# Sixteen seven-product blocks instead of thirteen, eight-wide channel runs, and engine orders written as lists, in a convolution and GELU kernel

## The chip, the cores and the metric

One core of a Trainium2 chip runs the kernel. The core has a matrix engine (TensorE, "PE" in the profile, with weight loads as "PEld"), VectorE (DVE), ScalarE (ACT), GpSimd (POOL), and a sync engine (SP) that issues transfers. Each engine works through its own queue in order and waits on semaphores for the others. The metric is the device time of one execution in microseconds (us).

## The reference, cut to what matters

x has 8 sequences of 4096 rows with 192 channels. Eight heads of 24 channels have seven taps each, which are normalised by a softmax. A causal convolution along the rows is followed by a two-layer product with an exact GELU between the layers:

```python
w = exp(weight - max); w = w / (sum(w) + 1e-9)        # [8 heads, 7 taps]
conv[b, s, c] = sum_k w[head(c), k] * x_pad[b, s + k, c]   # 6 zero rows ahead
h = conv.reshape(32768, 192) @ w_in                   # 192 x 2048
out = gelu_exact(h) @ w_out                           # 2048 x 192
```

## The kernel before, in words

The 32768 rows are two halves of 16384, which are worked on side by side: partitions 0 to 63 hold channels of the first half, 64 to 127 those of the second. A partition holds three of the 192 channels (NP = 3). A half is cut into 35 blocks: six of 256 rows (0 to 5), then 29 of 512 rows (6 to 34). So `win` holds W_in with three rows per partition, and each product with it takes three matmuls.

For one block n the stages are these:

- SP loads x rows into `xin` (`load`), one of three buffers, and stores results (`store`). Its queue alternates: load of block n+4, store of block n-1.
- DVE turns `xin` into `xT`, channels on partitions, by 32x32 transposes (`trans`, L800). Partition j holds the channels 3j, 3j+1, 3j+2, so the transpose reads every third element of a row of `xin`. POOL copies the last six rows of the block before it into the head of `xT` (`halo`, L723).
- The convolution is seven taps over 128 x 1536 elements. Tap 0 is a plain scaling, in three pieces on ACT (`first_tap`, L938; blocks 7 and 8 have it on DVE). Taps 1 to 6 are DVE multiply-adds into `acc` (`conv`, L827). The last one writes `xc` in bf16.
- TensorE forms the first product, 16 slices of 128 hidden channels for both halves, into two PSUM buffers `hp` (`mm1`, L1066). Four quadrants of 64x64 run side by side.
- ACT applies GELU to each slice and writes `gT` (L974).
- TensorE forms the second product for block n-1, between the slices of the first product of block n. DVE transposes the result back into `osb`.

The second product has two forms for blocks 6 to 33. A plain block (`mm2_t`, L1150) multiplies two row halves and two chunk parities of `gT` with three groups of 64 output channels: 12 products of 16 matmuls of 512 columns, 192 in all. A seven-product block (the list ST, `mm2_s`, L1202) replaces the eight products of two of the output groups by seven (P1 to P7), of sums of `gT` and of weights; the third group has D1, D2, E1, E2 (with pieces e1, e2). Together that is 11 products. The sums S1, Dn and S4 are made by DVE in `st_add`, S3 partly by DVE and partly by accumulating DMA transfers (`st_dma`, L545), which POOL issues. S3 overwrites a quarter of `gT`. After the product, ACT copies pieces of the PSUM banks X, D, Y and V to SBUF (`st_copy`: p5, p1, e, u, p3, -u, -g), DVE combines them (`st_post`: k0, k3, k4) and transposes the result (`st_evac`: ev). The tiles for this are `p5s`, `gsm`, `uu` and `tq`. The four banks of `ob` are handed from block to block (`BK`, `release`).

In the kernel before, ST holds every other block from 9 to 33: 13 blocks, each between two plain ones. The order on TensorE inside a seven-product block comes from TILES, which gives each quadrant its products. EVENTS merges the four orders by the time that each takes, counted in products: 5.5 in all. Some matmuls are marked to raise a semaphore (DONE): the last one of a product, and those after which the other row half takes over the same bank (SWITCH).

The order on DVE is a plan of transposes and taps by block, with side work put between them at fixed places (`AT_ST`, `at_ev`). ACT's copies stand at fixed slices (`AT_COPY`), its first taps too (`TAPS`). DVE's plan for block n runs about while TensorE works on block n-1.

Of the kernel before, what the change touches and what calls it, by code (L numbers as in the profile page):

```python
# [5 lines left out]
ALU = mybir.AluOpType  # L6
# [5 lines left out]
def bass_lightweight_conv__then__act_gelu_exact_kernel(  # L12
# [42 lines left out]
    DQ = D // 2  # L55

# [15 lines left out]
    ST = [m for m in range(M0 + 3, M1) if m % 2 == 1]  # L72
    K0 = {n: i for i, n in enumerate([4, 5, 6, *range(9, NB)])}
# [48 lines left out]
    with es:  # L122
# [61 lines left out]
        S_K0 = sem("S_K0")  # L184
        S_WT = sem("S_WT")
        S_ST = sem("S_ST")
# [3 lines left out]
        S_AD = [sem("S_AD%d" % q) for q in range(2)]  # L190
# [50 lines left out]
        def wait_pc(e, n, p):  # L241
# [11 lines left out]
            n: [(0, 0, 2), (0, 2, 1)] * (n not in K0) + [(k, 0, NP) for k in range(1, KS)]  # L253
            for n in range(NB)
            if n not in PC
        }
        FQ = F // 8
# [55 lines left out]
        def wait_banks(t, m, g):  # L313

            k = G0[m] + g
            if m < M0:
                if k >= 2:
                    t.wait_ge(S_EVA, k - 1)
            elif g % 2:
                t.wait_ge(S_GELU, SL0[NB] - 1 + g // 2)  # L320
            else:
                for b in LAST[g : g + 2]:
                    t.wait_ge(*release(OWNER[b], b))
# [42 lines left out]
        def evac_t(v, m, j):  # L366
# [22 lines left out]
            (0, 0): "P1 D1 e2 e1 D2 P6 P2", (1, 0): "D1 P1 P2 e2 e1 D2 P6",  # L389
            (0, 1): "P5 P7 E2 E1 P4 P3", (1, 1): "E2 P7:2 P5 P7:6 P3 E1 P4",  # L390
# [3 lines left out]
        EVENTS = []  # L394
        for (hf, cg), names in TILES.items():
            at, done = 0.0, {}
            for u in names.split():
                u, k1 = (u.split(":") + ["8"])[:2]
                k0 = done.get(u, 0)
                d = SPAN.get(u, (0, TB))[1] / TB  # L400
                for k in range(k0, min(8, k0 + int(k1))):
                    EVENTS.append((at, hf, cg, u, k))
                    at += d / 8
                    done[u] = k + 1
            assert abs(at - 5.5) < 1e-6 and all(k == 8 for k in done.values())
        EVENTS.sort(key=lambda q: (round(q[0], 4), q[1], q[2]))
        GROUP = {}
        for e, (at, hf, cg, u, k) in enumerate(EVENTS):
            name = {"D": "DE", "E": "DE", "e": "Ea"}.get(u[0], u)
            GROUP[name] = e  # L410
        DONE = {GROUP[name] for name in NE}
        SWITCH, last = {}, {}
        for e, (at, hf, cg, u, k) in enumerate(EVENTS):
            p = last.get((UNIT[u][0], cg))
            if p is not None and EVENTS[p][1] != hf:
                SWITCH[e] = p
                DONE.add(p)
            last[UNIT[u][0], cg] = e
        FIRST = {}
        for e, (at, hf, cg, u, k) in enumerate(EVENTS):  # L420
            FIRST.setdefault((UNIT[u][0], cg), e)
        DONE.discard(len(EVENTS) - 1)
        DONE = sorted(DONE)
# [3 lines left out]
        def st_done(e, m, name):  # L427
            if GROUP[name] == len(EVENTS) - 1:
                e.wait_ge(S_MM2, MMC[m + 1])
            else:  # L430
                e.wait_ge(S_ST, len(DONE) * ST.index(m) + DONE.index(GROUP[name]) + 1)

        COPIES = ("p5", "p1", "e", "u", "p3", "-u", "-g")
        AT_COPY = {
            "p5": (1, 6), "p1": (1, 8), "e": (1, 14), "u": (2, 0), "p3": (2, 2), "-u": (2, 6), "-g": (2, 10),
        }

        def ac(m, name):

            return len(COPIES) * ST.index(m) + COPIES.index(name) + 1  # L440

        POSTS = ("k0", "k3", "k4")

        def dp(m, name):

            return len(POSTS) * ST.index(m) + POSTS.index(name) + 1

        SUMS = {"S1": (0, 4, 6, 8), "S3": (6, 8), "Dn": (0, 4, 8), "S4": (0, 4, 8)}

        def sa(m, name, k):  # L450

            return (len(SUMS[name]) - 1) * ST.index(m) + [k < q for q in SUMS[name][1:]].index(True) + 1

        AT_ST = [
            (2, 1, 0, "S1", 0), (2, 1, 2, "Dn", 0), (2, 1, 4, "S4", 0), (2, 1, 6, "S1", 1),
            (2, 2, 2, "S1", 2), (2, 2, 4, "S3", 0), (2, 3, 0, "Dn", 1), (2, 4, 0, "S4", 1),
            (2, 5, 0, "k0", 0), (3, 1, 0, "ev", 2),
            (3, 6, 0, "k3", 0), (4, 1, 1, "ev", 1), (4, 1, 5, "k4", 0), (4, 2, 0, "ev", 0),
        ]

        def at_ev(n):

            if n == M0:
                return [(3, 1, 3), (3, 2, 1), (3, 2, 3)]
            return [(3, 1, 3), (3, 2, 1), (3, 2, 3)]
# [3 lines left out]
        for n in range(M0, M1):  # L469
            if n not in ST:  # L470
                SIDE += [((n + at[0], *at[1:]), "ev", n, j) for j, at in enumerate(at_ev(n))]
            else:
                SIDE += [((n + d, o, r), name, n, q) for d, o, r, name, q in AT_ST]
        SIDE.sort(key=lambda q: q[0])
        EV = {}
        for _, name, n, j in SIDE:
            if name in ("ev", "evac"):
                EV[n, j] = EVC[M0 - 1] + len(EV) + 1

        def release(m, b):  # L480
# [4 lines left out]
            if k == "X":  # L485
                return S_AC, ac(m, "p3")
# [5 lines left out]
        for m in range(M0, M1):  # L492
            for b in BK[m].values() if m in ST else BK[m]:
# [819 lines left out]
```

## Time and profile before

| what | value |
| --- | --- |
| median of 3 runs | 669.04 us (668.91 to 669.47) |
| profiled execution | 667.87 us, its span 666.1 us |
| PE busy | 661.4 us, 99% of the span |
| DVE busy | 600.7 us, 90% |
| ACT busy | 610.8 us, 92% |
| POOL busy | 47.6 us, 7% |
| GELU on ACT (L974) | 510 of 1.022 us |
| DVE taps (L827, 128 x 1536, into acc) | 145 of 1.811 us |
| input transposes (L800, 128 x 1536) | 29 of 2.369 us |
| DMA engines, mean | 96 GB/s |

The span reaches from the first to the last instruction of the profiled execution. Busy time is the time in which an engine has at least one instruction under way, and an instruction's row gives its count and mean duration. Instructions of DVE and ACT overlap a little, so the start-to-start time can be less than the duration. "Idle before" names what ended the wait of an engine. In a row of TensorE by order of time, a group of 12 matmuls is one slice of the first product.

### The profile page before, as it was taken

Reading aid. Unit: us, or ns where it says so; the run is one execution under the profiler, and the core shown is the slowest. Engines: PE = TensorE matmul, PEld = TensorE weight load, DVE = VectorE, ACT = ScalarE, POOL = GpSimd, SP = SyncE. Lnnn points to the kernel's source line nnn. Section 1 sums busy time; section 2 is a strip of 40 time slices with the busy share of each in tenths; the row PEclk is TensorE's granted clock in tenths of the full one; section 3 lists DMA queues with packets and bytes.
Section 4 is the critical chain, followed back from the end, with each engine's and each line's share of the span. In section 5 each row is a group of like instructions: output and inputs, shape, how many; then the busy total and the mean of one; then the engine's idle time right before and its main releaser. Section 6 shows DMA issues by size and latency. Waiting matters only on the chain.

```text
span 666.1 us, 27567 instructions
## 1 busy us (share of the span) xinstructions
PE 661.4 (99%) x12712; PEld 516.4 (78%) x12712; DVE 600.7 (90%) x510; ACT 610.8 (92%) x720; POOL 47.6 (7%) x87
## 2 busy tenths in 40 slices
PE   8999999999999999999999999999999999999998
PEld 8999655557667787877878778787787878878787
DVE  6979999799999999999999999999999999999632
ACT  8999988889999999999999999999999999999884
POOL 7000000010000100001010010100001000010100
PEclk9999999999999999999999999999999999999999
DMA  9735334243081461905529073370824719151233
GB/s 159 165 89 130 65 69 97 72 93 79 18 197 29 107 135 34 203 7 127 114 41 201 3 163 78 62 179 2 191 50 91 151 29 192 22 118 29 56 90 97
DMA packets 137028, 63.92 MB, mean 96 GB/s; under 512 B 126800, under 2 KB 133520, under 8 KB 136912
## 3 DMA queue, kind: packets, MB, share of 16 engines
q1 hardware_dynamic: 129136, 49.37, 33.2%
q0 software_dynamic: 6656, 12.19, 10.1%
q8 instruction: 100, 1.64, 1.1%
q10 hardware_dynamic: 1120, 0.59, 0.3%
q14 instruction: 16, 0.13, 0.1%
HBM read 28.31 MB, written 25.17 MB: 80 GB/s over the span
## 4 chain that ended last, share of the span: by engine, by line
PE 99%; ACT 0%; DVE 0%; DMA 0%; issue 0%; ACTq 0%
PE hp L1066 50%; PE ob L1150 23%; PE ob L1202 18%; PE ob L1106 5%; PE ob L1258 1%; PE hp L1258 1%; PE ob L1011 0%; DMA wsb<-in_weight_dram 0%; PE ob L1066 0%; ACT dg L912 0%; DVE wcol L772 0%; ACT xc L237 0%; ACT osb L347 0%; ACT wex L899 0%; ACT xTb L269 0%
## 5 line engine op out<-in xcount | busy, mean ns | idle before, releaser
L974 ACT ACTIVATE gT<-hp 128x1024 bf16<-128x1024 f32 x510 | 513.0, 1022 | 43.0 <-PE hp L1066 35.7
L1066 PE MATMUL hp<-xc,win 64*64 64x512 bf16 (+2 forms) x6036 | 438.4, 366 | 0.2
L1066 PEld LDWEIGHTS hp<-xc,win 64*64 64x64 bf16 (+1 forms) x6036 | 247.2, 106 | 73.0 <-ACT gT L974 4.6
L827 DVE SCALAR_TENSOR_TENSOR acc<-xT,wcol,acc 128x1536 f32<-128x1536 f32 (+1 forms) x165 | 282.9, 1714 | 10.6 <-ACT acc L938 7.3
L1150 PE MATMUL ob<-gT,wot 64*64 64x512 bf16 x2880 | 205.6, 376 | 0.0
L1202 PE MATMUL ob<-gT,wot 64*64 64x512 bf16 x832 | 158.0, 376 | 0.0
L1150 PEld LDWEIGHTS ob<-gT,wot 64*64 64x64 bf16 x2880 | 112.1, 107 | 43.3
L1202 PE MATMUL ob<-gT,wst 64*64 64x512 bf16 (+2 forms) x832 | 144.0, 323 | 0.0
L1202 PE MATMUL ob<-s_S,wot 64*64 64x128 bf16 (+2 forms) x624 | 89.9, 305 | 0.0
L800 DVE STREAM_TRANSPOSE xT<-xin 128x1536 f32<-128x1536 f32 (+2 forms) x39 | 76.2, 1963 | 3.8 <-DMA xin<-in_x_dram 1.4
L1202 PEld LDWEIGHTS ob<-gT,wst 64*64 64x64 bf16 x832 | 68.5, 107 | 10.7
L1202 PEld LDWEIGHTS ob<-gT,wot 64*64 64x64 bf16 x832 | 63.9, 107 | 1.5
L938 ACT ACTIVATE acc<-xT,wcol 128x512 f32<-128x512 f32 (+1 forms) x87 | 61.2, 703 | 0.0
L827 DVE SCALAR_TENSOR_TENSOR xc<-xT,wcol,acc 128x1536 bf16<-128x1536 f32 (+1 forms) x33 | 56.7, 1720 | 0.8
L1202 PE MATMUL ob<-s_S,wst 64*64 64x512 bf16 x208 | 57.4, 376 | 0.0
L1202 PE MATMUL ob<-s_Dn,wst 64*64 64x512 bf16 x208 | 57.4, 376 | 0.0
L1202 PEld LDWEIGHTS ob<-s_S,wot 64*64 64x64 bf16 x624 | 50.2, 107 | 8.6
L545 POOL DMA_DIRECT2D gT<-gT x26 | 22.4, 861 | 318.1 <-DVE s_S L559 318.1
L1106 PE MATMUL ob<-wout,gT 64*128 64x192 bf16 x768 | 41.9, 243 | 0.0
L1106 PEld LDWEIGHTS ob<-wout,gT 64*128 64x128 bf16 x768 | 35.1, 94 | 3.3
L373 DVE STREAM_TRANSPOSE osb<-ob 128x512 f32<-128x512 f32 x45 | 31.1, 694 | 6.2 <-PE ob L1150 6.2
L559 DVE TENSOR_TENSOR s_S<-gT 128x1024 bf16<-128x1024 bf16 (+1 forms) x39 | 32.6, 837 | 1.4 <-ACT gT L974 1.3
(78 smaller groups left out, 322.6 us busy)
## 6 DMA issues: line engine op xcount, KB each, us to landing
out_dram<-osb SPq DMA_DIRECT2D x124, 192.0 KB, 3.6
xin<-in_x_dram SPq DMA_DIRECT2D x116, 192.0 KB, 4.2
gT<-gT POOLq DMA_DIRECT2D x13, 512.0 KB, 4.6
gT<-gT POOLq DMA_DIRECT2D x13, 256.0 KB, 3.3
xin<-in_x_dram SPq DMA_DIRECT2D x18, 96.0 KB, 2.5
wout<-in_moe_w_out_dram POOLq DMA_DIRECT2D x4, 192.0 KB, 4.7
win<-in_moe_w_in_dram POOLq DMA_DIRECT2D x4, 96.0 KB, 4.3
win<-in_moe_w_in_dram POOLq DMA_DIRECT2D x2, 192.0 KB, 4.5
```

The source lines that it names most:

```text
L373: v.transpose(osb_t(m, j), bank(BK[m][j])).then_inc(S_EV)
L545: e.dma_start(quad(m, 1, 0, k, k1 - k), quad(m, 0, 0, k, k1 - k), accum_op=ALU.add).then_inc(S_AD[q], 16)
L559: ins = v.tensor_tensor(t("S1"), quad(m, 1, 0, k, n), quad(m, 1, 1, k, n), ALU.add)
L800: v.transpose(out, src).then_inc(S_TR)
L827: ins = v.scalar_tensor_tensor(dst, src, wk, a, op0=ALU.mult, op1=ALU.add)
L938: a.activation(out=acc[n % 2][:, p * TB : p * TB + w], in_=ap(xT[n % 2], p * XW + HX, [[NP * XW, 128], [1, w]]), func=AF.Copy, scale=wcol[ ...
L974: a.activation(out=ap(gT[n % 2], (i % 2 * NF + i // 2) * TB if n in ST else i * c * 2 * w, dst), in_=ap(ob, 2 * TB, [[4 * TB, 128], *src[1 ...
L1066: ins = t.matmul(hbuf(u, slice(fo, fo + fw), o, w), ap(win, f1, [[NP * F, 64], [2, fw]]), xc[n % 2][r, p * TB : p * TB + w], start=(p == 0 ...
L1106: ins = t.matmul(bb[sub], gT[m % 2][r, c0 : c0 + 128], wout[r, CH[sub][i] * C : (CH[sub][i] + 1) * C], start=(ph == 0 and k == 0), stop=(p ...
L1150: ins = t.matmul(bank(BK[m][j], slice(64 * h, 64 * h + 64), w), ap(wot, 64 * hf * NF * C + CH[h][i] * C + 64 * j, [[NF * C, 64], [1, 64]]) ...
L1202: ins = t.matmul(bank(BK[m][bk], slice(64 * cg, 64 * cg + 64))[:, c0 : c0 + w], wt_, x, start=(e == mine[0]), stop=(e == mine[-1] or e in ...
L1258: ins = t.matmul(banks(m, g)[h], gT[m % 2][:, c0 : c0 + 128], wout[:, CH[h][i] * C : (CH[h][i] + 1) * C], start=(i == 0), stop=(i == NF - 1),)
```

## The change

There are four parts.

1. ST becomes 9, 10, 12, 14, 15, 17, 19, 20, 22, 24, 25, 27, 29, 30, 32, 33: 16 blocks, with six pairs side by side. TILES has two orders: "S" (the one of before) behind a seven-product block, "N" behind a plain one. Four more matmuls are marked, which tell when a sum has been read (READ), since the next block may overwrite it (`st_read`). Banks are released by column half.
2. From block 7 on (NR) partition j holds channels in runs of eight: 24 consecutive channels are three runs of eight over eight partitions. The input transpose then reads runs of eight elements. W_in is loaded again in that layout, into the same tile, by 24 transfers from POOL (`win_again`) in four groups. A group waits until block 6 has read its columns, and TensorE waits for the groups at slices 0, 4, 8 and 10 of block 7. The six halo rows of block 7 get an own load and a transpose, since block 6 has the old layout.
3. In the ten blocks behind a plain one the first half of Dn is made by two DMA transfers (a copy "cp", then an accumulate "Dn"), not by DVE. p5 and p1 become one ACT copy over 128 partitions (p15). The staging tiles alternate (`gs`, `tqs`).
4. The order of DVE (LIST), ACT (SLOT) and POOL (GLIST) is written out entry by entry from block 9 on. Blocks 13, 18, 23, 28 and 33 have two thirds of tap 0 on DVE.

```diff
-    ST = [m for m in range(M0 + 3, M1) if m % 2 == 1]
+    RUN, NR = GRP // NP, 7
+    ST = [m for m in [9, 10, 12, 14, 15, 17, 19, 20, 22, 24, 25, 27, 29, 30, 32, 33] if m < M1]
+    TYPE = {m: "S" if m in ST else "N" for m in range(-4, NB + 4)}
+    LIST = {
...
+        16: "t17 k4.0.12 1 2 3 S1.0.14 ev.0.13 4 k3.0.12 ev.0.12 S1.1.14 5 ev.1.12 S1.2.14 ev.1.13 Dn.1.14 S3.2.14 ev.2.13 6",
+        17: "1 S4.0.14 S4.1.14 2 k0.0.14 t18 S1.0.15 S1.1.15 3 ev.2.14 4 Dn.0.15 S1.2.15 S3.2.15 5 Dn.1.15 k4.0.14 S4.0.15 S4.1.15 6",
+        18: "0 k0.0.15 k3.0.14 t19 ev.0.14 1 ev.1.14 2 ev.2.15 3 4 5 6",
...
+    SLOT = {
...
+        11: "0:p3.9 2:u.9 4:-g.9 6:p15.10 8:f2.13 9:f0.14 11:-u.9 14:e.10 15:f1.14",
...
+        16: "0:p3.14 2:u.14 4:-g.14 6:p15.15 8:-u.14 12:f0.19 14:e.15",
...
-            (0, 0): "P1 D1 e2 e1 D2 P6 P2", (1, 0): "D1 P1 P2 e2 e1 D2 P6",
-            (0, 1): "P5 P7 E2 E1 P4 P3", (1, 1): "E2 P7:2 P5 P7:6 P3 E1 P4",
+            "N": {
+                (0, 0): "P1 D1 e1 e2 D2 P6 P2", (1, 0): "D1 P1 P2 e1 e2 D2 P6",
+                (0, 1): "P5 P7 E1 E2 P4 P3", (1, 1): "E1:4 E2:4 P7:2 P5 P7 P3 E2 E1 P4",
+            },
+            "S": {
+                (0, 0): "P1 D1 e2 e1 D2 P6 P2", (1, 0): "D1 P1 P2 e2 e1 D2 P6",
+                (0, 1): "P5 P7 E2 E1 P4 P3", (1, 1): "E2 P7:2 P5 P7:6 P3 E1 P4",
+            },
...
+            for name, who in (("S1", ("P5", "E1", "e1")), ("Dn", ("P6",)), ("S4", ("P3",))):
+                cuts = (0, 4, 6, 8) if name == "S1" else (0, 4, 8)
+                for q, (k0, k1) in enumerate(zip(cuts, cuts[1:])):
+                    READ[name, q] = max(e for e, v in enumerate(EVENTS) if v[3] in who and k0 <= v[4] < k1)
+                    DONE.add(READ[name, q])
...
+        BYDMA = {'N': 'S3.0 S3.1 Dn.0', 'S': 'S3.0 S3.1'}
...
+            if name == "cp":
+                e.wait_ge(S_GELU, SL0[m] + 2 * k1)
+                st_read(e, m, "Dn", q)
+                if ST.index(m):
+                    e.wait_ge(*summed(ST[ST.index(m) - 1], "S4", k))
+                e.dma_start(d, quad(m, 0, 0, k, k1 - k)).then_inc(S_AD["cp.%d" % q], 16)
+            else:
+                e.wait_ge(S_AD["cp.%d" % q], SUM_AT[m, "Dn", q][1])
+                e.wait_ge(*summed(m, "S1", k1 - 1))
+                e.dma_start(d, s1, accum_op=ALU.add).then_inc(S_AD["Dn.%d" % q], 16)
...
-                    "p5": (p5s[UP, :], xb(UP)),
-                    "p1": (gsm[LO, :], xb(LO)),
+                    "p15": (gs(m)[:, :], bank(BK[m]["X"])),
...
+        GLIST = (
+            "halo.10 halo.11 cp.0.9 halo.12 S3.0.9 Dn.0.9 S3.1.9 S3.1.10 S3.0.10 "
...
+            "S3.1.19 halo.23 S3.1.20 S3.0.20 halo.24 cp.0.22 Dn.0.22 S3.1.22 S3.0.22 "
...
+            def win_again(k):
+                g.wait_ge(S_MM1, SL0[NR - 1] + (4, 8, 14, 16)[k])
+                c0 = 2 * FQ * (0, 2, 1, 3)[k]
+                for hf in range(2):
+                    for p in range(NP):
+                        g.dma_start(
+                            ap(win, (64 * hf * NP + p) * F + c0, [[NP * F, 64], [1, 2 * FQ]]),
+                            ap(wint, RUN * p * F + c0, [[GRP * F, 8], [F, RUN], [1, 2 * FQ]]),
+                        ).then_inc(S_WR[k], 16)
+
+            for n in range(3, 10):
+                halo(n)
+                for k in {NR: (0,), NR + 1: (1, 2, 3)}.get(n, ()):
+                    win_again(k)
...
-                        [[TB // 32 * DQ, 128], [1, NP], [DQ, w // 32], [NP, 32]],
+                    run = [[1, NP], [DQ, w // 32], [NP, 32]]
+                    if n >= NR:
+                        run = [[RUN, NP], [DQ, w // 32], [GRP, 4], [1, RUN]]
+                    src = ap(xin[n % NX], 0, [[TB // 32 * DQ, 128], *run])
...
+                if n == NR and i in (0, 4, 8, 10):
+                    t.wait_ge(S_WR[(0, 4, 8, 10).index(i)], 32 * NP)
```

In LIST an entry is a tap (1 to 6, 0 for the two thirds of tap 0), a transpose t with its block, or a piece with part and block: "S1.0.14" is the first part of S1 of block 14. SLOT gives the slice of the block ahead of which ACT does a first tap (f0 to f2) or a copy.

## The prediction

> **What bounds the kernel now.** I read the page first (busy shares and the chain that ended last), then the waits, then TensorE's instructions in order of time, to find where a block begins, and last the busy time by block.
>
> ```profile
> PE 661.4 (99%) x12712; PEld 516.4 (78%) x12712; DVE 600.7 (90%) x510; ACT 610.8 (92%) x720; POOL 47.6 (7%) x87
> PE 99%; ACT 0%; DVE 0%; DMA 0%; issue 0%; ACTq 0%
> ```
>
> The chain is TensorE alone, so only fewer matmul slots or a new TensorE wait can move the end. In order of time, a block n starts where the second product changes from L1150 (plain block before it) to L1202 (seven-product block before it):
>
> ```profile
> 286.86 0.87 PE L1066 MATMUL hp<-xc,win 64*64 64x512 bf16 x12
> 307.58 0.87 PE L1066 MATMUL hp<-xc,win 64*64 64x512 bf16 x12
> 327.47 0.87 PE L1066 MATMUL hp<-xc,win 64*64 64x512 bf16 x12
> ```
>
> By block (columns: length, then busy us of PE, PEld, DVE, ACT, POOL, clock, DMA):
>
> ```profile
> 286.86:307.58 20.72, 20.72 (x390) 16.28 (x384) 19.55 (x16) 19.84 (x24) 1.25 (x2) 1.00 0.14 28
> 307.58:327.47 19.89, 19.89 (x407) 16.39 (x401) 19.67 (x17) 18.62 (x23) 1.30 (x3) 1.00 0.83 174
> ```
>
> A block whose predecessor is plain takes 20.72 us, one behind a seven-product block 19.89. The clock is full. DVE is busy 39.2 of the 40.61 us of a pair, ACT 38.5: both are hidden, with little to spare. The rows that price the change, from the groups with shapes kept apart:
>
> ```profile
> L800 DVE STREAM_TRANSPOSE xT<-xin 128x1536 f32<-128x1536 f32 x29 | 68.6, 2369 | 2.3
> L827 DVE SCALAR_TENSOR_TENSOR acc<-xT,wcol,acc 128x1536 f32<-128x1536 f32 x145 | 262.6, 1811 | 6.1 <-ACT acc L938 3.4
> L565 DVE TENSOR_TENSOR s_Dn<-gT,s_S 128x2048 bf16<-128x2048 bf16 x26 | 31.2, 1198 | 0.1
> L373 DVE STREAM_TRANSPOSE osb<-ob 128x512 f32<-128x512 f32 x45 | 31.1, 694 | 6.2 <-PE ob L1150 6.2
> ...
> L772 DVE STREAM_TRANSPOSE wcol<-wnt 32x32 f32<-32x32 f32 x4 | 0.8, 202 | 0.1
> ```
>
> **TensorE: three more seven-product blocks.** ST grows from 13 to 16. Each exchange turns a 20.72 us block into a 19.89 us one: 0.83 us. By slots it is the same: a plain product is 192 matmuls of 512 columns in four quadrants, the seven-product form 208 shorter and full ones worth 176, so 4 of 96 slots go, 4 x 20.72/96 = 0.86. I take the measured 0.83: 3 x 0.83 = 2.50 us. The new tile order N (E1 and E2 swapped, in two halves) puts every bank switch at the same place in the block, 15 as before, so I cost it at nothing; what could change is only which sums must be ready first.
>
> The form has 24 semaphore marks on matmuls instead of 20 (four new ones tell when a sum has been read). What 17 more marks and 15 switches cost now: a block of 92 slots should take 92 x 20.72/96 = 19.86 us, and takes 19.89. That is at most 0.03/17 = 1.8 ns each, and 16 x 4 new marks cost 0.11 us at the most. [...]
>
> **DVE: does the extra work fit?** Per five blocks the new pattern has three seven-product blocks. From the pair's 39.2 us I take out 12 taps at 1.817 and 2 input transposes at 2.416 (rows of that pair), and 3 plain evacuations at 0.63 (0.69, less their overlap): a seven-product block costs DVE 39.2 - 21.8 - 4.8 - 1.9 = 10.7 us beside its taps and transpose. Five blocks now: 30 taps 54.5, one two-thirds first tap back on DVE 0.77, two plain blocks' evacuations 3.8, three times 10.7, less two half Dn sums that go to DMA (2 x 1.1): 29.9. That is 89.0 us plus five input transposes. TensorE gives 2 x 20.72 + 3 x 19.89 = 101.1.
>
> The transposes decide. Before, they read every third element. No row shows runs of eight at a step of 24. Upper end: nothing gained, 2.37 each. Lower end: the rate of the transposes whose source is contiguous. (0.694 - 0.202)/(512 - 32 elements) = 1.025 ns an element, so 0.20 + 1504 x 0.001025 = 1.74 us. I take 1.75, since inside a run the read is contiguous and eight is most of it. A gain below that rate is excluded by the contiguous rows. DVE then needs 97.7 of 101.1 us (96.6%, against 96.5% before); with the upper end 100.8 (99.7%). [...]
>
> **DVE's order.** The lists set it by hand. I added them up, list 9 on from the end of convolution 8 (100.28), each entry at its start-to-start time of the trace (tap 1.85 before another tap, 1.73 otherwise; half sums 1.10, quarter sums 0.58, evacuations 0.63, k0/k3/k4 0.61), tap 6 not ahead of its xc buffer, sums not ahead of their GELU. Held against block starts (103.77, 124.49, then 20.72 or 19.89 each), every convolution ends before its block starts: 9 to 18 us ahead mostly, 4.9 at block 32, 3.2 at block 34. Input transposes end 0.5 to 10 us before the ACT slot that takes the first tap. With 2.37 us a transpose some come 0.3 to 0.9 late there.
>
> The tightest single place is the side-by-side pair. Bank V of the second block is the first one's Y, freed by k4. k4 waits for the -g copy: slot 4 of ACT (5.0 us into the block; the copy 0.65), then k4 itself 0.61: about 6.5. The first e2 or e1 stands at 2/5.5 of the block: 7.2. Room 0.6 us, at six pairs; what waits behind is the whole TensorE queue.
>
> **ACT.** p5 and p1 become one copy over 128 partitions (0.59 instead of 0.59 + 0.58), and 13 first taps fall per five blocks instead of 15. ACT's worst block is 11: 16 GELUs at 0.91, three first taps at 0.61, six copies (3.4): 19.8 of 19.89 us. TensorE has two hp buffers, so ACT may run about 0.9 us late. I cost it at 0; without that cover each late tenth goes straight into the end.
>
> **POOL and its DMAs.** Twenty more transfers of 512 KB (cp and Dn for the ten blocks behind a plain one), in order with halos and S3. Rows of the existing ones (groups, DMA issues, the tile gT):
>
> ```profile
> L545 POOL DMA_DIRECT2D gT<-gT x26 | 22.4, 861 | 318.1 <-DVE s_S L559 318.1
> gT<-gT POOLq DMA_DIRECT2D x13, 512.0 KB, 4.6
> ...
> DMA to landing us min/median/max: 3.2/4.4/6.3
> ```
>
> P7 needs S3.0 at 0.75/5.5 of the block, 2.7 us in. Worst of the second blocks is 25: S1.0 ends 2.6 us before its block by my sum, so 5.3 us are there for 4.6. Worst of the chained ones (22): cp can go at 398, lands 402.2; Dn takes the queue till 406.1, S3.1 (1.3) and S3.0 (2.5) follow: 410.0 against 410.6. Dn.0 itself has over 10 us. DMA is busy 47% in a pair, so a load or store may overlap; I take 0.
>
> **W_in reload.** 24 transfers of 64 KB, POOL 0.70 to 0.86 each. Block 6 runs 67.3 to 83.0, 0.98 a slice; the four groups may start at 71.2, 75.2, 81.1, 83.0. With 6 issues each, one behind another, the last goes out at 88.9 to 91.3 and lands 4.3 to 4.6 later: 93.2 to 95.9. Block 7 needs it at slice 10: 83.0 + 10 x 1.3 = 96.0. Halo 8 waits behind the first group (to 76.4) and is wanted at 89; halo 9 behind the rest (92) and is wanted after 100. Cost 0, at worst 2 us once. Four small loads and one transpose for the halo of block 7 (0.3 us of DVE at 68) lie under TensorE's early blocks.
>
> **Sum.** The profiled execution took 667.87 (span 666.1 and 1.8 around it): 667.87 - 2.50 + 0.11 = 665.5. The runs' median is 669.04, 1.17 above it; in those terms 666.6. A change under 0.2% (1.34 us: the runs span 668.91 to 669.47) can't be told from none.
>
> **Rivals.**
> - Scattered waits. Rooms of 0.4 to 1 us (k4, ev.2, S3.0) are within what a sum by rows can miss. Some sixteen blocks losing 0.1 us: 668.2. For it: the rooms are thin; against: before runs at the same DVE share without a TensorE wait of note.
> - Side transfers come late, and the kernel is slower. S3.0 in the chained blocks stands behind cp and Dn on one queue, and loads and stores share the engines. The slowest accumulate took 6.3 us against the 512 KB median of 4.6, 1.7 more. If two of the three in the chain meet that, less some 0.9 us of room, TensorE waits 2.5 us in a block; five blocks are chained so (12, 17, 19, 22, 29). Two of them: 5 us, 671.6; all: 12. It decides for slower from 0.39 us a block, (2.5 + 1.34)/10, over the ten cp blocks. Against: by my sum a store or load starts beside the chain in 17 and 19 alone.
> - Runs of eight read no faster: DVE at 99.7%. By the list sum every convolution is still in time, but seven first taps come 0.3 to 0.9 us late to ACT; taken whole, 7 x 0.55 = 4 us: 670.6. Against: the two contiguous rows.
> - The reload stalls block 7 by 2 us: 668.6.
> [...]
>
> **How the numbers follow.** Full gain 0.63, scattered waits 0.15, late transfers 0.11, transposes as before 0.05, reload 0.03, marks 0.03. Predicted: the likeliest, 666.6. Its own range is 665.9 (slot arithmetic 3 x 0.86, and the runs' spread) to 667.4. With scattered waits, reload and marks up to 669.6 the range holds 0.84. Faster by over 0.2% (under 667.7): the first case and a third of the scattered one, reload and marks: 0.70. Within: the rest of those and half the transposes: 0.17. Slower: late transfers and half the transposes: 0.13.
>
> **What the changed profile would show.** Right: 192 fewer L1150-type matmuls per exchanged block, blocks still 20.72 and 19.89, input transposes near 1.75 us, PEld's waits on anything but ACT nil. Wrong: TensorE blocks of more than 20.8 us; a wait of PE on gT by DMA (late S3), on DVE gsm or osb (banks), or on win at block 7; transposes above 2 us.

## The result: slower by 1.3%

The changed kernel takes 677.01 us (median of 5 runs, 676.61 to 680.81), the kernel before 669.04 beside it. The ratio is 1.0128, with a 95% interval of 1.0112 to 1.0145. The prediction was 666.6 us, faster with a chance of 0.70. It was wrong by 10.4 us and in the sign.

The profiled execution of the changed kernel is the slowest of its five: 680.81 us, with a span of 678.6 against 666.1 before. Its page, the busy line, two lines of the DMA queues and the chain that ended last:

```profile
PE 665.2 (98%) x12760; PEld 467.9 (69%) x12760; DVE 604.3 (89%) x539; ACT 607.4 (90%) x715; POOL 89.9 (13%) x137
...
q0 software_dynamic: 13856, 26.62, 19.8%
q8 instruction: 100, 1.64, 1.1%
...
PE 62%; DVE 15%; DMA 10%; issue 7%; ACT 3%; SPq 2%; POOL 1%; DVEq 0%; POOLq 0%
```

Before, 99% of the chain was TensorE. Now a third of it is VectorE, transfers and what the page calls issue (time in which an engine waits for nothing that the profile shows). None of the three busy engines has become fuller: VectorE's share of the span fell from 90% to 89%, ScalarE's from 92% to 90%. POOL's rose from 7% to 13%, and its own transfers moved 26.62 MB instead of 12.19.

Read in order of time as in the prediction, 27 blocks (7 to 33) have a length each. In the interval of block n TensorE works off the first product of block n and the second of block n-1, so the form of n-1 decides it. I call excess what a block takes over 19.89 us (behind a seven-product block) or 20.72 (behind a plain one). Before, the excess of the 27 blocks is 0.0 us. After, it is 14.1:

| blocks | second product of | excess, us |
|---|---|---|
| 10 | S9, first of a pair | 2.44 |
| 13, 18, 20, 23, 30 | S12, S17, S19, S22, S29: S3.0 behind Dn.0 on POOL's list | 0.91, 0.96, 3.12, 1.27, 0 |
| 15, 25, 28, 33 | S14, S24, S27, S32: S3.0 ahead of Dn.0 | 0.21, 0, 0, 0.13 |
| 11, 21 | S10, S20, second of a pair: S3.1 ahead of S3.0 | 1.00, 1.23 |
| 16, 26, 31 | S15, S25, S30, second of a pair: S3.0 first | 0.38, 0.23, 1.08 |
| 14, 17, 24, 27 | a plain block | 0.39, 0.15, 0.13, 0.38 |
| 7, 8, 9, 12, 19, 22, 29, 32 | a plain block | 0 to 0.06 |

The account closes: 14.1 of excess, less 2.5 for three exchanges, plus 1.1 for a late start of block 7 (84.1 instead of 83.0; in the profiles below it lies between 83.0 and 85.1), less 0.3 in the tail, is 12.4, and the spans differ by 12.5.

Three blocks of the changed kernel (columns: length, then busy us of PE, PEld, DVE, ACT, POOL, clock, DMA share, GB/s): block 19 (plain), 20 (S19) and 21 (S20).

```profile
334.32:355.06 20.74, 20.74 (x392) 15.65 (x388) 20.19 (x16) 19.52 (x24) 2.73 (x5) 1.00 0.18 49
355.06:378.06 23.00, 20.47 (x407) 15.30 (x404) 18.70 (x17) 17.97 (x21) 3.61 (x4) 1.00 0.92 189
378.06:399.19 21.13, 20.43 (x408) 14.56 (x404) 19.37 (x19) 19.17 (x23) 1.13 (x1) 1.00 0.36 81
```

At full clock, no engine is busy for the 23.00 us of block 20: TensorE is idle for 2.5 us of it, and VectorE for over 4. It is a block of waits, and the DMA engines are busy 92% of it. The waits of the whole run (us in total, times, longest):

```profile
POOL s_Dn L677 <- DMA s_Dn<-gT: 17.8, 6, 4.7
DVE xT L968 <- DMA xin<-in_x_dram: 13.7, 10, 3.4
...
PEld hp L1242 <- ACT gT L1149: 10.3, 37, 1.0
...
PE ob L1376 <- DMA gT<-gT: 6.0, 7, 1.8
...
DVE s_S L699 <- DMA s_Dn<-s_S: 4.5, 2, 3.0
...
PEld ob L1376 <- DMA gT<-gT: 3.0, 3, 1.4
...
PEld ob L1376 <- ACT uu L740: 2.7, 3, 1.2
...
PEld ob L1376 <- DVE gT L693: 2.0, 2, 1.6
```

None of TensorE's waits on DMA, on uu and on VectorE's gT was there before. Its wait on ScalarE's GELU was, in the kernel before:

```profile
PEld hp L1066 <- ACT gT L974: 4.6, 25, 0.2
```

Two of the blocks show how it comes about. In block 19, POOL's list for S19 in order of time (start, duration, line):

```profile
346.39 0.56 POOL L673 DMA_DIRECT2D s_Dn<-gT  x1 [22.87 <-ACT gT L1149]
351.64 0.85 POOL L677 DMA_DIRECT2D s_Dn<-s_S  x1 [4.69 <-DMA s_Dn<-gT]
...
352.86 0.84 POOL L662 DMA_DIRECT2D gT<-gT  x1
354.95 0.86 POOL L662 DMA_DIRECT2D gT<-gT  x1 [1.25 <-DVE s_S L690]
```

The copy cp.0 can't go before half of the GELUs are done, 12.1 us into block 19. POOL then waits 4.69 us for it to land: fifteen of the 16 engines that move it have raised its semaphore by 349.6 us, the last at 351.4. So Dn.0 starts at 351.64 and S3.0 behind it at 352.86. Between 346 and 364 us the landings of these transfers (KB, us from issue to landing) were, behind 5.0 for cp.0:

```profile
s_Dn<-s_S POOLq DMA_DIRECT2D x1, 512.0 KB, 4.6
gT<-gT POOLq DMA_DIRECT2D x1, 512.0 KB, 7.7
gT<-gT POOLq DMA_DIRECT2D x1, 256.0 KB, 9.2
```

S3.0 lands at 360.5 us. TensorE wants it 2.7 us into the block, at 357.8.

In block 10 two things hold S9. The first is the same chain: cp.0 lands 8.0 us after its issue, Dn.0 and S3.1 stand behind it on POOL's list, and S3.1 lands at 153.4 us. The second is VectorE's list. TensorE, then VectorE, each in order of time:

```profile
153.44 0.40 PE L1376 MATMUL ob<-gT,wst 64*64 64x512 bf16 x1 [0.92 <-DMA gT<-gT]
...
155.83 0.40 PE L1376 MATMUL ob<-gT,wst 64*64 64x512 bf16 x1 [1.12 <-DVE gT L693]
```

```profile
152.22 1.23 DVE L699 TENSOR_TENSOR s_S<-gT,s_Dn 128x2048 bf16<-128x2048 bf16 x1 [2.99 <-DMA s_Dn<-s_S]
...
153.99 1.18 DVE L696 TENSOR_TENSOR s_Dn<-gT,s_S 128x2048 bf16<-128x2048 bf16 x1
155.10 0.68 DVE L693 TENSOR_TENSOR gT<-gT 128x1024 bf16<-128x1024 bf16 x1
```

S4.0 (L699) waits 2.99 us for the Dn.0 that comes by DMA. Behind it in the list stands S3.2 (L693), for which TensorE then waits 1.1 us, and its weight load 1.6.

### The profile page after: what moved, and what is told of

The parts are those of the page before. It is cut to its first block, busy times and chain, and to the rows that moved or that the text cites. A ratio compares the mean times of both kernels' runs of the same rounds, so it can differ in the third digit from the quotient of the medians.

```text
span 678.6 us, 27828 instructions
## 1 busy us (share of the span) xinstructions
PE 665.2 (98%) x12760; PEld 467.9 (69%) x12760; DVE 604.3 (89%) x539; ACT 607.4 (90%) x715; POOL 89.9 (13%) x137
## 3 DMA queue, kind: packets, MB, share of 16 engines
q0 software_dynamic: 13856, 26.62, 19.8%
## 4 chain that ended last, share of the span: by engine, by line
PE 62%; DVE 15%; DMA 10%; issue 7%; ACT 3%; SPq 2%; POOL 1%; DVEq 0%; POOLq 0%
PE hp L1242 31%; PE ob L1376 18%; PE ob L1327 10%; DVE acc L343 8%; DMA gT<-gT 5%; DMA xin<-in_x_dram 2%; ACT gT L1149 2%; DVE xT L968 2%; PE ob L1282 2%; DVE xc L343 1%; DMA s_Dn<-gT 1%; SPq L796 1%; DMA s_Dn<-s_S 1%; DVE s_S L690 1%; PE ob L1432 1%
## 5 line engine op out<-in xcount | busy, mean ns | idle before, releaser
L1242 PEld LDWEIGHTS hp<-xc,win 64*64 64x64 bf16 (+1 forms) x6036 | 230.5, 105 | 97.3 <-ACT gT L1149 10.3
L1376 PE MATMUL ob<-gT,wst 64*64 64x512 bf16 (+2 forms) x1024 | 182.3, 323 | 7.9 <-DMA gT<-gT 6.0
L1376 PE MATMUL ob<-s_S,wot 64*64 64x128 bf16 (+2 forms) x768 | 120.4, 305 | 0.0
L1327 PEld LDWEIGHTS ob<-gT,wot 64*64 64x64 bf16 x2304 | 77.9, 107 | 49.1 <-DVE osb L766 0.8
L1376 PEld LDWEIGHTS ob<-gT,wst 64*64 64x64 bf16 x1024 | 87.7, 107 | 21.5 <-issue 4.0
L1376 PEld LDWEIGHTS ob<-gT,wot 64*64 64x64 bf16 x1024 | 81.6, 107 | 13.8
L1376 PE MATMUL ob<-s_S,wst 64*64 64x512 bf16 x256 | 72.2, 377 | 0.0
L968 DVE STREAM_TRANSPOSE xT<-xin 128x1536 f32<-128x1536 f32 (+2 forms) x39 | 59.3, 1531 | 14.3 <-DMA xin<-in_x_dram 13.7
L1376 PE MATMUL ob<-s_Dn,wst 64*64 64x512 bf16 x256 | 70.8, 376 | 0.0
L878 POOL COPY xT<-xT 128x18 f32<-128x18 f32 x29 | 24.2, 833 | 169.9 <-DVE xc L343 157.7
L699 DVE TENSOR_TENSOR s_S<-gT,s_Dn 128x2048 bf16<-128x2048 bf16 x32 | 38.5, 1217 | 5.1 <-DMA s_Dn<-s_S 4.5
```

Of the source, the lines that this page charges most:

```text
L699: ins = v.tensor_tensor(t("S4"), quad(m, 0, 1, k, n), t("Dn"), ALU.add)
L878: g.tensor_copy(dst, src).then_inc(S_HALO)
L968: v.transpose(out, src).then_inc(S_TR)
L1242: ins = t.matmul(hbuf(u, slice(fo, fo + fw), o, w), ap(win, f1, [[NP * F, 64], [2, fw]]), xc[n % 2][r, p * TB : p * TB + w], start=(p == 0 ...
L1327: ins = t.matmul(bank(BK[m][j], slice(64 * h, 64 * h + 64), w), ap(wot, 64 * hf * NF * C + CH[h][i] * C + 64 * j, [[NF * C, 64], [1, 64]]) ...
L1376: ins = t.matmul(bank(BK[m][bk], slice(64 * cg, 64 * cg + 64))[:, c0 : c0 + w], wt_, x, start=(e == mine[0]), stop=(e == mine[-1] or e in ...
```

## Experiments: which part costs

Four theories. **A**: the side transfers are late because stores and loads share the 16 DMA engines with them. **B**: VectorE's list is too full or in a bad order. **C**: the x loads come late (13.7 us of waits). **D**: cp, Dn and S3 one behind another on POOL's queue are too long by themselves. I give each run's excess from its one profile beside its time; the times carry the verdicts. A profile is one execution, and it can lie off the median: that of the changed kernel by 3.8 us above it, that of VectorE's places alone by 1.6 us below. Ratios are to the kernel before, measured beside each run.

**The runs of eight and the reload alone.** The kernel before with its thirteen blocks and lists, and only the runs of eight channels and the reload of W_in added (`run = [[1, NP]...` in the transposition, `win_again`, as in the diff).

> The kernel before with runs of eight from block 7 on and the reload of W_in alone: 13 seven-product blocks, the orders of before. If that part is innocent: input transposes near 1.77 us, no wait of TensorE at block 7, time 668.5 to 669.7 (DVE gains 17 us off the path). If the reload stalls TensorE: 670 to 672.

668.68 us; ratio 0.9997 (0.9987 to 1.0006). The excess is 0.0, and VectorE has 16 us less work than before:

```profile
PE 661.8 (99%) x12712; PEld 510.3 (77%) x12712; DVE 584.7 (88%) x511; ACT 611.5 (92%) x720; POOL 64.3 (10%) x111
```

The time is what was expected of a part that costs nothing. It is worth nothing by itself either, since VectorE was hidden. The loss is in the rest of the change: the sixteen blocks, their sums by DMA and their lists.

**Dn.0 back on VectorE.**

```diff
-        BYDMA = {'N': 'S3.0 S3.1 Dn.0', 'S': 'S3.0 S3.1'}
+        BYDMA = {'N': 'S3.0 S3.1', 'S': 'S3.0 S3.1'}
```

and Dn.0 in VectorE's lists of those ten blocks, cp and Dn out of POOL's.

> The changed kernel, but the first half of Dn of the ten blocks behind a plain one is a DVE add again (1.10 us each) in the place ahead of S4.0, and the 20 transfers cp and Dn are gone from POOL's queue. Theory A (the added side transfers and S3 are late because they share the DMA engines with loads and stores; a late Dn.0 holds DVE at S4.0, a late S3 holds TensorE): the wait of S4 on Dn by DMA is zero, TensorE's waits on gT by DMA fall from 9.0 us to under 3, and the time falls to 668 to 672 although DVE has 11 us more to do. Theory B (DVE's lists are too full or in a bad order): 11 us more of DVE work makes it slower, 680 or more. Theory C (x loads come late): about 677, with DVE's wait on xin still above 10 us.

676.53 us; ratio 1.0114 (1.0097 to 1.0131). TensorE's waits on gT by DMA fall from 9.0 us (the 6.0 and 3.0 above) to 1.4, yet the excess is still 11.1, spread over more blocks: VectorE is now busy 616.2 us, and TensorE's weight loads wait 12.7 us for GELUs and 3.0 for uu, instead of 10.3 and 2.7. Block 10 falls from 2.4 to 0.7. No theory had both the time and the waits: A had the waits but expected 668 to 672 us, B expected 680 or more, and C had the time but expected over 10 us of waits on x, where 6.9 are left. The transfers are not the whole cause, and taking all ten sums off the queue mostly moved the waits.

**A quarter of the stores.** `for q in range(1)` instead of four in the stores of blocks 6 to 33.

> The changed kernel with only one of the four store transfers of blocks 6 to 33 (three quarters of those output rows' pieces are left out), so SP's queue and the DMA engines carry 16 MB less. Theory A by contention: side transfers land nearer their undisturbed 4.2 us, TensorE's waits on gT fall below 3 us, time 667 to 671. Theory A without contention (the chain cp, Dn, S3 on one queue is too long by itself): 674 to 677. Theory B: 676 to 677. Theory C: 668 to 672, since the loads stand behind the stores on SP, with DVE's wait on xin going to zero.

674.88 us; ratio 1.0092 (1.0076 to 1.0107); excess 8.5. The stores that are gone are worth 0.0036 of the time, 2.4 us (0.9 to 3.9 by the two intervals). That is where a chain that is too long without contention was expected, 674 to 677. Block 20 stalls 3.7 us without them too. But block 10 is clean here, with its order as it was: cp.0 of S9 lands 4.5 us after its issue instead of 8.0. (The five kernels that keep both this order and the stores lose 2.1 to 2.4 us there.) Contention (A) is a part, and in block 10 a condition. Why cp of S19 is slow even so shows in the DMA view of this kernel, 340.9 to 345.5 us, where no load and no store runs:

```profile
q0 software_dynamic: 144, 0.52, 28.8%
q8 instruction: 1, 0.02, 1.7%
...
s_Dn<-gT POOLq DMA_DIRECT2D x1, 512.0 KB, 4.2
```

This copy takes 4.2 us; the median of such copies in the changed kernel is 2.9. By the packets' records fourteen of the 16 engines were done 2.4 to 2.5 us after its issue, one at 2.8 and the last at 3.8; the completion came 0.4 us later. The records don't name the engine of a packet, but the last one's first packet began at 343.04 us, just where the 16 KB instruction packet on q8 ended (343.06).

**Loads ahead of stores.** From block 12 on, each store stands one place later in SP's list, behind the next load.

> The changed kernel with SP's stores one place later in its queue from block 11 on (load n+4, then store n-2), so a load no longer stands behind the store of a seven-product block. Theory C: DVE's wait on xin (13.7 us) goes to near zero and the time falls by 5 us or more, to 668 to 672. Theory A: DVE's wait on xin falls, but the time stays at 675 to 678, as TensorE's waits on gT stay.

678.46 us; ratio 1.0147 (1.0132 to 1.0162). VectorE's waits on x fall from 13.7 to 3.0 us and the time does not fall. So theory C is out: those waits did not set the time.

**S3.0 earlier on POOL's list.** All three kernels only reorder POOL's list. "Chain" puts S3.0 ahead of Dn.0, "pair" puts S3.0 ahead of S3.1:

```diff
-  cp.0.19 Dn.0.19 halo.22 S3.0.19 S3.1.19      (chain: S12, S17, S19, S22, S29)
+  cp.0.19 S3.0.19 Dn.0.19 halo.22 S3.1.19
-  S3.1.20 S3.0.20                              (pair: S10, S20)
+  S3.0.20 S3.1.20
```

Both:

> The changed kernel with one thing altered, the order of POOL's transfers: S3.0 goes ahead of Dn.0 in the five chained blocks (12, 17, 19, 22, 29), and S3.0 ahead of S3.1 in the pairs 10 and 20. Theory D (the chain of side transfers is too long: each waits for the slowest of 16 DMA engines, which an instruction fetch or a load can hold back by more than a microsecond): TensorE's waits on gT by DMA fall from 9.0 us to under 4, blocks 20 and 23 lose 3 to 4 us of their 4.4 us of stall, 11 and 21 lose 1 to 2 of 2.2, and the time falls by 4 to 7 us to 670 to 673. Theory B (DVE's own lists are too full): 675 to 677, the waits only move.

Chain alone:

> The changed kernel with S3.0 ahead of Dn.0 in the five chained blocks alone. Theory D: 672 to 674, with blocks 20 and 23 near 19.9 to 20.3 us and blocks 11 and 21 still about 21. Theory B: 675 to 677.

Pair alone:

> The changed kernel with S3.0 ahead of S3.1 in the pairs 10 and 20 alone. Theory D: 675 to 676, with blocks 11 and 21 about 1 us shorter and block 20 still near 23. Theory B: 676 to 677.5.

Both: 674.91 us, ratio 1.0081 (1.0051 to 1.0111), excess 8.8. Chain: 676.69, 1.0109 (1.0091 to 1.0128), 11.3. Pair: 675.6, 1.0091 (1.0070 to 1.0111), 8.3. With both, blocks 18, 20 and 23 lose no more than 0.12 us each and block 21 only 0.17. But where Dn.0 now comes later a block that was clean stalls. Block 30 (S29) of the kernel with both orders has an excess of 1.9 us:

```profile
DVE s_S L699 <- DMA s_Dn<-s_S: 2.1, 1, 2.1
PEld ob L1376 <- DVE s_S L690: 1.0, 1, 1.0
```

S4.0 waits for Dn.0, and S1 behind it on VectorE is late for TensorE. It is VectorE's part of block 10 once more. The kernel with the chain order alone has the same 1.9; the one without it has 0.1.

By the times, D missed twice: it expected 670 to 673 us for both orders and 672 to 674 for the chain alone, whose interval overlaps that of the changed kernel. The pair alone came within its range, but block 20, expected to stay near 23 us, fell to 21.1 without having been touched. What holds is local: where S3.0 was moved ahead, blocks 20, 21 and 23 are nearly clean. Each block has its own right order: in S19 S3.0 is urgent, in S29 Dn.0 is.

**Dn.0 on POOL itself**, by its own adder instead of two transfers, with the orders of both.

```diff
-                e.dma_start(d, s1, accum_op=ALU.add).then_inc(S_AD["Dn.%d" % q], 16)
+            e.tensor_tensor(d, quad(m, 0, 0, k, k1 - k), s1, ALU.add).then_inc(S_AD["Dn.%d" % q])
```

> The changed kernel with the order of transfers of the run with S3.0 first, and the half sum Dn.0 of the ten blocks computed by POOL's own add (2048 bf16 elements) instead of the two transfers cp and Dn. DVE has no more work than in the changed kernel and the DMA engines 10 MB less. If POOL's reads leave DVE alone: waits on gT by DMA under 3 us, time 668 to 672. If POOL and DVE hold each other: POOL's add 4 us or more, DVE's multiply-adds beside it longer than 1.81 us, time 674 to 684.

701.58 us; ratio 1.0478 (1.0451 to 1.0504), worse than any theory had it. The groups, with shapes kept apart:

```profile
L673 POOL TENSOR_TENSOR s_Dn<-gT,s_S 128x2048 bf16<-128x2048 bf16 x10 | 46.4, 4642 | 0.0
...
L343 DVE SCALAR_TENSOR_TENSOR acc<-xT,wcol,acc 128x1536 f32<-128x1536 f32 x145 | 278.0, 1917 | 5.8 <-ACT acc L1103 3.4
...
L686 DVE TENSOR_TENSOR s_S<-gT 128x1024 bf16<-128x1024 bf16 x32 | 32.4, 1013 | 1.5 <-ACT gT L1145 1.4
```

With ten adds of 4.64 us on POOL some of VectorE's own operations are longer: taps into acc a mean of 1.92 instead of 1.81, S1's quarter sums 1.01 instead of 0.68, and VectorE's total 639.4 us instead of 604.3. That is 3.5 us of VectorE's time for each of the ten adds, three times what the sum costs there (1.21).

**Each order where it helped.** Chain for S17, S19, S22 only, the pair order for S10 and S20, and three places on VectorE (Dn.0 of S9 by VectorE's own add, with it and S3.2 ahead of S4.0; S1.0 of S9; S1.0 of S30):

```diff
-  cp.0.9 halo.12 S3.0.9 Dn.0.9 S3.1.9
+  halo.12 S3.0.9 S3.1.9
-  S1.2.9 ev.1.8 S4.0.9 ev.2.8 Dn.1.9 S3.2.9
+  S1.2.9 ev.1.8 Dn.0.9 S3.2.9 S4.0.9 ev.2.8 Dn.1.9
-  1 2 3 S1.0.9 ev.0.8 4 5
+  1 2 S1.0.9 3 ev.0.8 4 5
-  1 k0.0.29 t33 2 S1.0.30 S1.1.30
+  1 k0.0.29 S1.0.30 t33 2 S1.1.30
```

> Changed kernel with the orders that helped, at the places where they helped: S3.0 ahead of Dn.0 on POOL's list in blocks 17, 19 and 22 (not 12 and 29), S3.0 ahead of S3.1 in blocks 10 and 20; Dn.0 of block 9 on VectorE and ahead of its S4.0, its S1.0 one tap earlier; S1.0 of block 30 ahead of a transposition that waits for x. All 16 seven-product blocks stay. If the stalls were rooms of the side transfers and two places in VectorE's list (theories B and D), the excess over the ideal block lengths falls from 14.1 us in the changed kernel's profiled run (8.3 to 8.8 with one or both orders alone) to 2 to 5 us, and the time to 667 to 670 us. If the total load of the transfers or of the engines sets it (theory A, or a VectorE that is simply too full), the stalls move to other blocks and the time stays at 672 us or above.

668.93 us (12 runs); ratio 1.0000 (0.9989 to 1.0011). All sixteen blocks are there, and with ten entries of the lists moved or dropped 8.6 us are gone, as expected if the stalls were a matter of places. The excess is 3.5. Blocks 19, 20 and 21 of this kernel, in the columns of above:

```profile
327.96:348.70 20.74, 20.74 (x392) 15.64 (x388) 20.19 (x16) 19.52 (x24) 3.06 (x5) 1.00 0.32 75
348.70:368.78 20.08, 20.08 (x407) 16.98 (x404) 18.31 (x17) 17.80 (x21) 3.60 (x4) 1.00 1.01 210
368.78:388.88 20.10, 20.10 (x408) 14.45 (x401) 19.48 (x19) 18.98 (x23) 1.13 (x1) 1.00 0.27 65
```

In block 20 the transfers are denser than in the changed kernel (210 against 189 GB/s; the DMA share adds up the times of packets, so it can pass 1), and the block stalls for 0.2 us instead of 3.1. What counted was which of them came first.

**The VectorE places alone**, POOL's list as in the changed kernel.

> The changed kernel with VectorE's places alone mended: block 9's Dn.0 on VectorE ahead of its S4.0, its S1.0 one tap earlier, S1.0 of block 30 ahead of a transposition; POOL's list as in the changed kernel. If the stalls are independent, those of blocks 10, 11 and 31 (2.4, 1.0 and 1.1 us) mostly go and those of blocks 18, 20, 21 and 23 (1.0, 3.1, 1.2 and 1.3) stay: 672.5 to 674.5 us. If the late start in block 9 is what makes the later blocks late, 669 to 671; if the order on POOL alone matters, 676 to 677.

675.02 us; ratio 1.0081 (1.0064 to 1.0098), excess 7.5. Blocks 10 and 31 are clean, as expected; 20, 21 and 23 keep 2.0, 1.1 and 1.4, and the time is 0.5 us above what was expected. Two blocks did not do what was expected: 11 kept 1.5 us, and 18 went clean untouched. The two groups of stalls can be removed apart from each other. Alone, the places are worth 0.0047 of the time (3.1 us, 1.5 to 4.7 by the intervals), and POOL's two orders as much (0.9 to 5.4); together, without the orders of S12 and S29, 8.6. Block 10 is mended by three moves in S9 at once. The first of them, Dn.0 on VectorE, leaves 0.7 us of its 2.4 in the run that did it in all ten blocks; the other two are not taken apart.

Since a profile is one execution, the case for the order on POOL's list is how a block does over the kernels in which its place is the same (the changed kernel, a quarter of the stores, loads first, both orders, chain, pair, places, each order where it helped):

| block | its transfers in the order of the changed kernel: excess, us | S3.0 moved ahead: excess, us |
|---|---|---|
| 20 (S19) | 1.2 to 3.7 in 5 kernels | 0 to 0.2 in 3 |
| 23 (S22) | 0.7 to 1.4 in 5 | 0 to 0.1 in 3 |
| 21 (S20) | 1.1 to 1.4 in 5 | 0.2 in 3 |
| 11 (S10) | 1.0 to 1.6 in 5 | 0.4 to 0.6 in 3 |
| 30 (S29) | 0 to 0.1 in 6 | 1.9 in 2 |
| 13 (S12) | 0 in 4, 0.9 and 1.0 | 0.9 and 1.4 |
| 18 (S17) | 0 in 4, 1.0 in the changed kernel | 0 to 0.2 in 3 |

In the first five blocks the two columns do not overlap, so there the order decides. In blocks 13 and 18 it is not shown to: they stall in some executions and not in others with the same list.

**The mended kernel with a quarter of the stores.**

> The same mended order with only one of four stores of blocks 6 to 33, which leaves three quarters of those output pieces out. It prices what contention with the stores still costs once the orders are mended. If the rooms are wide enough, within 0.7 us of the mended order alone; if contention (theory A) holds the rest, 1.5 to 3 us less.

669.07 us; ratio 1.0001 (0.9991 to 1.0012); excess 2.0. Once the orders are right, three quarters of the store traffic are worth nothing that can be measured in the time (within 1.0 us). So most of what contention cost, it cost through the bad order: that late transfers meet the stores is the likely reason, and not shown by itself.

**Where is the predicted gain?** The mended kernel only ties with the one before. More moves at places that still stalled, four of sums and evictions and three of ScalarE's pieces:

```diff
-  k0.0.24 2 t28 3 S1.0.25 ev.2.24
+  k0.0.24 2 S1.0.25 t28 3 ev.2.24
-  halo.27 halo.28 S3.0.25
+  halo.27 S3.0.25 halo.28
-  S1.0.10 S1.1.10 5 ev.2.9 t13
+  S1.0.10 S1.1.10 ev.2.9 5 t13
-  S1.2.32 ev.1.30 S4.0.32 Dn.1.32 S3.2.32 ev.2.31
+  S1.2.32 ev.1.30 S3.2.32 Dn.1.32 S4.0.32 ev.2.31
-  14: "... 7:f0.17 ..."  27: "... 9:f0.30 ... 12:f1.30"  28: "2:f2.30 ..."
+  14: "... 12:f0.17"     27: "... 14:f0.30"              28: "1:f1.30 2:f2.30 ..."
```

> The mended order with six more moves, each at a place where its trace still shows a stall: S1.0 of block 25 ahead of a transposition, and S3.0 of block 25 ahead of the halo copy on POOL's list (block 26, 0.67 us); the last piece of block 9's eviction ahead of a tap (block 11, 0.61); S3.2 of block 32 ahead of S4.0 (block 33, 0.25); three of ScalarE's tap-0 pieces moved out of blocks 14 and 27, where its calls are bunched (0.30 and 0.40). If each stall is a matter of its own place, 1.3 to 1.9 us of the 3.5 us that are left go, and the time is 667.0 to 667.7 us, just below the kernel before. If VectorE and ScalarE are simply full, the stalls move and the time stays within 0.5 us of 668.9.

668.71 us; ratio 0.9993 (0.9982 to 1.0003); excess 3.1. The time missed the 667.0 to 667.7 that separate stalls would have given, and stayed where moved stalls would leave it. Blocks 26, 27 and 33 got better by 1.1 us together, and block 25, clean until then, lost 1.1. Its waits:

```profile
PEld hp L1243 <- ACT gT L1150: 1.6, 2, 1.4
...
ACT acc L1108 <- DVE xT L969: 1.1, 1, 1.1
```

S1.0.25 was moved ahead of the transposition of block 28. ScalarE's first-tap piece of block 28 waited 1.1 us for that transposition, the GELUs stood behind it, and TensorE behind them. With that move taken back and two more for block 11:

> The twice mended order with its own mistake undone: the transposition of block 28 is again ahead of S1.0 of block 25 (ScalarE's tap-0 piece of block 28 waited 1.1 us for it and held the GELUs, 1.14 us in block 25), and two moves for block 11 (an eviction subtraction ahead of S4.0 of block 10, one tap-0 piece later). If the sixteen seven-product blocks pay what was predicted once nothing is late (three more blocks, 0.83 us each, 2.5 us below the kernel before), an excess of 1.4 to 1.9 us is left of 3.1 and the time is 0.6 to 1.1 us below the kernel before. If the gain is eaten elsewhere (another block, the head or the tail), it stays within 0.5 us of it.

668.8 us; ratio 1.0002 (0.9991 to 1.0013); excess 3.4. This gain did not come either. Block 25 is down to 0.2; block 15 has 0.7, where the two kernels before had none, though nothing in it was changed. The rest is many small waits, and most are of one kind: TensorE's weight loads on GELU, 42 times, 12.0 us (25 times and 4.6 us before). Most of those 12.0 us are hidden, since the whole excess is 3.4. The last run makes ScalarE's first-tap pieces shorter, with their number and order kept:

```diff
-                w = WS[n]
+                w = 64 if n >= 9 else WS[n]
```

> The three times mended order with ScalarE's tap-0 pieces of blocks 9 and later only 64 columns wide instead of 512, which leaves seven eighths of those pieces out. ScalarE's calls keep their order and number, and get shorter by some 20 us in all (about 70 pieces of 0.72 us). In the mended orders 42 to 43 waits of TensorE for a GELU, 12 us of weight loads, are the bulk of what is left of the excess (3.1 to 3.5 us). If ScalarE's bunched calls are what eats the last of the gain, the excess falls under 1.2 us and the time lies 1.5 to 2.5 us below the mended order's 668.7, near the 666.6 that was predicted for the changed kernel. If it is lost at another place, the time stays within 0.7 us of the mended order.

667.7 us; ratio 0.9984 (0.9975 to 0.9993); excess 2.0. The group and the wait in this kernel, from the groups and from the waits:

```profile
L1108 ACT ACTIVATE acc<-xT,wcol 128x64 f32<-128x64 f32 x68 | 22.9, 340 | 0.4 <-DVE xT L969 0.4
```

```profile
PEld hp L1243 <- ACT gT L1150: 5.9, 24, 0.4
```

ScalarE is busy 589.7 us instead of 605.8. TensorE's waits for it are back near those of before, and about 1.1 us come back, less than the 1.5 expected at the least. Three exchanges pay 2.5; the 2.0 us of excess that stay in this profile eat most of that. They sit at VectorE's evictions (0.5 in block 24, 0.25 in block 12), at uu in block 11 (0.7) and in waits of 0.1 to 0.2. Whether a better order could free these too was not tried.

## Why the prediction was wrong, step by step

- **Blocks of 20.72 and 19.89, 0.83 us an exchange: right.** Where nothing waits, the changed kernel's blocks last 20.72 to 20.74 and, behind a seven-product block, 19.87 to 19.88 (25, 28, 30). The order N cost nothing by itself.
- **The marks at 0.11 us at most: right.** Where nothing waits, the blocks with 24 marks take 19.87 to 19.88 us, those with 20 took 19.89 before. No run shows the larger cost of the marks that the chance of 0.03 stands for.
- **The transposes at 1.75: right.** The group of the whole input transpositions in the changed kernel:

```profile
L968 DVE STREAM_TRANSPOSE xT<-xin 128x1536 f32<-128x1536 f32 x29 | 51.7, 1787 | 10.8 <-DMA xin<-in_x_dram 10.3
```

  1.79 us, against 2.37 at a step of three. The gain is spent on the sums of the three added blocks, as the step had it: VectorE is busy 604.3 us, 600.7 before.
- **The reload at 0: right.** Block 7 takes 20.75 us.
- **"Dn.0 itself has over 10 us": wrong, the first failed step.** It names neither the reader of Dn.0 nor what is queued behind that reader. S4.0 on VectorE reads Dn.0, and VectorE takes its list in order: S3.2 stands behind S4.0, and TensorE wants that. In S9, Dn.0 landed 15.1 us after cp.0 was issued. This cost 1.1 to 1.6 us of the 2.4 of block 10 here (the rest is the late S3.1), and 1.9 in block 30 as soon as Dn.0 was moved back.
- **"410.0 against 410.6", the chain cp, Dn, S3 at 0: wrong, the second failed step.** It added up 4.2, 3.9, 1.3 and 2.5 us, for which it shows no rows, to about 12 us, and left 0.6 us of room to the due time. In S22, the block that it worked out, S3.0 landed 13.7 us after the issue of cp, 1.1 more than sum and room together, and block 23 lost 1.3. In S19 cp took 5.0 us instead of 4.2, S3.0 landed 14.1 us after it, and block 20 lost 3.1. Over the run the 512 KB S3 landed in a median of 5.8 us, not 4.6, and the 256 KB ones in up to 9.2. "A load or store may overlap; I take 0" was the same error: by the run with a quarter of the stores it was about 2.4 us.
- **"I cost it at 0" for ScalarE: wrong in size.** Its calls bunch in blocks 14 and 27; the last run puts about 1.1 us on the length of its pieces.
- **The list sum of VectorE.** The convolutions came in time, as it said. The places that failed were others: sums for the second product in the same lists (S4.0 and S3.2 of S9, S1.0 of S30). The prediction had named the rooms of k4, ev.2 and S3.0.

The slower rival, late side transfers, had one mechanism and the condition right (0.39 us a block decides), and a chance of 0.11. It priced stalls of 2.5 us in two to five chained blocks. Of these, four lost 0.9 to 3.1 us, 6.3 of the 14.1 of excess. The rest lies outside what it named: block 10, where VectorE's list has a part, the second blocks of pairs (11 and 21, where S3.1 stood ahead of S3.0), and block 31 with S1.0 of S30. The rival of scattered waits came true underneath: the mended kernels keep 3.1 to 3.5 us in many small waits, twice the 1.6 that it priced, and that is why none of them shows the gain of 2.5 us. What frees them stays open, but for the 1.1 us of ScalarE's pieces. The steps costed at 0 with rooms of 0.4 to 1 us should have carried one likelihood of stalls together, not a small one each.

## What to carry to other kernels

When a transfer takes over a sum, price it at the engine that reads the result: write down the next two entries in that engine's list and who waits for them. On a shared in-order queue the urgent transfer goes first, and which one is urgent differs from block to block; here ten entries moved or dropped were worth 8.6 us, the whole loss. A room of 0.6 us under a chain of landings of 3 to 8 us was no cover here, and handing all ten sums to an engine that was 89% busy mostly moved the stalls.

## What the runs showed of the hardware

- A side transfer landed with the last of its 16 engines, and 16 KB packets of the instruction queue (100 in a run, before and after) seem to hold one back. In the changed kernel, the first and last engine of a 512 KB side transfer raised its semaphore 0.18 us apart (median of 12; at most 0.9, beside loads or stores) when no such packet ran between its issue and its landing, and 1.7 (median of 24; at most 4.2) when one did. S3.0 of S22 is one of these: fifteen engines had raised its semaphore by 423.0 us and the last at 424.5, and block 23 lost 1.3 us. No run took these packets away, so this is read from the records, not tested.
- An add of 128x2048 bf16 took POOL 4.64 us and VectorE 1.21, and with ten of them on POOL VectorE's own work was 3.5 us longer for each (639.4 us against 604.3).
- A transposition of 128x1536 floats that reads runs of eight took 1.79 us, one at a step of three 2.37.
